# Two tiles on the path of each layer: residual through TensorE, statistics from PSUM, and a limit of two query projections in PSUM

## The chip, the cores and the metric

One core of one Trainium2 chip. The metric is the device time of one execution in microseconds (us), the median of several runs. A profile ("look") is one further execution, with its own span.

## The reference

Two layers, each an attention with feature maps (no square score matrix) and a gated feed-forward. S = 2048 rows are 16 tiles of 128; D = 576; 32 heads of 18; the feed-forward is 4608 wide.

```python
def A(x):                      # attention of one layer
    q, k, v = heads(layernorm(x) @ wqkv)
    pq, pk = q @ w_phi, k @ w_phi                       # per head, 18 x 18
    phi_q = concat(softmax(pq), softmax(-pq))
    phi_k = concat(softmax(pk), softmax(-pk))
    kv, z = phi_k^T v, sum(phi_k)                       # over ALL rows
    return (phi_q @ kv) / (phi_q @ z + 1e-6) @ wo
def B(x):                      # feed-forward
    n = layernorm(x); return ((n @ w_gate) * (n @ w_up)) @ w_down
for layer in range(2):         # the same weights in both
    x = x + A(x);  x = x + B(x)
```

The sum over all rows in `kv` is what makes a barrier: no row can finish its attention before the last row's key features are in. From there to the first feed-forward matmul only the first two tiles count, because a feed-forward block takes two tiles.

## The kernel before

The kernel is written as many small threads, each yielding operations for one engine. A list scheduler, run when the kernel is built, picks the next ready operation of each engine by priority. So a change of one thread can move the others. The parts that matter here:

```python
# a tile's query projection: a filler for TensorE; two PSUM banks each
def t_qproj(self, L, st_):
    ...
    if st_ >= s.pqn[L - 1]:                  # 16: never true
        yield ("when", lambda: s.sc.open)
    gots = yield ("acqn", ["pb"], 2, True)   # two PSUM banks
    banks = [g_[1] for g_ in gots]
    yield from s.proj(st_, s.Wq, "Wq", banks)
    ... two ScalarE copies, banks given back ...

# key-value sums of layer 2: three groups, one bank asked for at a time
def t_kv(self, b):
    ...
    for bi in range(3):
        (_, bank), = yield ("acqn", ["pb"], 1)
        ... matmuls vx, dd -> bank;  DVE: kvacc += bank;  give bank back

# end of attention of a tile
def t_aout(self, L, st_):
    ...  # numerators: eT x BD; all three thirds of BD are waited for
    reads=[("eT", et)] + [("BD", bi) for bi in range(3)]
    ...  # DVE: den + 1e-6, 1/den, o = num / den, and 64 columns doubled
    ops.append(Op(130, ... tensor_copy(o[:, 576:640], o[:, 512:576]) ...))
    ...  # first two tiles: 5 transposes on TensorE, ScalarE copies them to oT
    yield from s.proj(st_, s.Wo, "Wo", banks, s.oT[:, oTb, :, :], ...)
    for h in range(2):    # residual on DVE
        ... tensor_tensor(xs, s.ps[:, bank, 0:288], xs, ALU.add) ...
    yield ("sig", ("x1", L, st_))
# then t_ln: bn_stats of x_sb (DVE), Ln and Exp for rstd (ScalarE), normalise
# (DVE, again 64 columns doubled), 5 transposes (TensorE), ScalarE copy to xT
```

The doubled columns exist because 576 is 4.5 times 128: a transpose of the last half block puts its 64 rows into both halves of the partitions, where the half-height matmuls of this kernel read them. "Half-height" is a matmul with 64 partitions on the contracting side; projections inside feed-forward blocks run in that form, 18 half-height matmuls in place of 10 full ones.

The names: DVE is VectorE; a "bank" is one of the eight PSUM buffers of the kernel's pool "pb", into which TensorE writes. Wq, Wk, Wv and Wo are weights, and "a Wq projection" is the multiplication of one tile by Wq. xT and oT are transposed tiles. kvacc gathers the key-value sums, BD is the matrix made of them, and the numerators are the matmuls with BD.

## Time and profile before

| | before |
|---|---|
| median of 3 runs | 1123.65 us (1119.85 to 1124.21) |
| span of the profiled run | 1118.2 us |
| TensorE busy | 1070.8 us, 96% |
| layer 1: numerators to first feed-forward matmul | 106.87 to 121.26 |
| layer 2: first Wq after the last down projection, first numerator, first feed-forward matmul | 620.16, 646.86, 659.52 |

In profile lines a row of the timeline is: start, duration, engine, line of the kernel, operation, output<-inputs, shapes, count; in square brackets the idle time of that engine just before, and what ended it. PEld is the weight load of TensorE. Rows of the busy table by stretches are: stretch, its length, busy us and instruction count of PE, PEld, DVE, ACT, POOL, then granted clock, DMA share, GB/s.

### The profile page before, as it was taken

Reading aid. Unit: us, or ns where it says so; the run is one execution under the profiler, and the core shown is the slowest. Engines: PE = TensorE matmul, PEld = TensorE weight load, DVE = VectorE, ACT = ScalarE, POOL = GpSimd, SP = SyncE. Lnnn points to the kernel's source line nnn. Section 1 sums busy time; section 2 is a strip of 40 time slices with the busy share of each in tenths; the row PEclk is TensorE's granted clock in tenths of the full one; section 3 lists DMA queues with packets and bytes.
Section 4 is the critical chain, followed back from the end, with each engine's and each line's share of the span. In section 5 each row is a group of like instructions: output and inputs, shape, how many; then the busy total and the mean of one; then the engine's idle time right before and its main releaser. Section 6 shows DMA issues by size and latency. Waiting matters only on the chain.

```text
span 1118.2 us, 33702 instructions
## 1 busy us (share of the span) xinstructions
PE 1070.8 (96%) x15258; PEld 832.8 (74%) x15320; DVE 596.7 (53%) x1206; ACT 375.1 (34%) x859; POOL 313.5 (28%) x333
## 2 busy tenths in 40 slices
PE   5787999999999999999999889999999999999998
PEld 3565786868687786869687668696969696969685
DVE  7898754647466564646453576453535353524231
ACT  6776631414233242414232443131313130402120
POOL 5595522414242432413220234121212030300000
PEclk9799999999999999999999999999999999999999
DMA  7952127273452626371523202727172726352504
GB/s 188 250 225 64 29 41 204 47 203 47 142 102 76 161 37 190 45 203 26 162 65 105 88 13 54 217 36 214 35 201 48 202 47 188 61 178 50 177 28 139
DMA packets 181034, 128.23 MB, mean 115 GB/s; under 512 B 99354, under 2 KB 179738, under 8 KB 179738
## 3 DMA queue, kind: packets, MB, share of 16 engines
q1 hardware_dynamic: 180890, 126.07, 43.6%
q8 instruction: 120, 1.97, 0.7%
q14 instruction: 24, 0.20, 0.1%
HBM read 100.73 MB, written 2.36 MB: 92 GB/s over the span
## 4 chain that ended last, share of the span: by engine, by line
PE 82%; DVE 11%; ACT 4%; DMA 1%; issue 1%; POOL 0%; SPq 0%; DVEq 0%; ACTq 0%
PE ps L1342 47%; PE ps L1412 21%; PE ps L943 6%; PE ps L1415 4%; PE ps L931 2%; DVE ss L1058 2%; PE ps L1230 1%; DVE dd L990 1%; PE ps L1111 1%; DVE hT L1390 1%; ACT hT L1388 1%; DVE mxmn L976 1%; DVE st L877 1%; DVE mxmn L971 1%; DVE x_sb L1278 1%
## 5 line engine op out<-in xcount | busy, mean ns | idle before, releaser
L1342 PE MATMUL ps<-xT,Wu 64*128 64x256 bf16 x4608 | 581.6, 269 | 0.2 <-DVE hT L1390 0.2
L1342 PE MATMUL ps<-xT,Wg 64*128 64x256 bf16 x4608 | 580.5, 269 | 0.8 <-ACT xT L913 0.8
L1342 PEld LDWEIGHTS ps<-xT,Wu 64*128 64x128 bf16 x4608 | 431.1, 94 | 23.7 <-DVE hT L1390 2.2
L1342 PEld LDWEIGHTS ps<-xT,Wg 64*128 64x128 bf16 x4608 | 426.8, 94 | 27.6 <-issue 3.3
L1388 ACT CAST hT<-ps 128x512 bf16<-128x512 f32 x288 | 168.3, 585 | 566.5 <-PE ps L1342 537.2
L1390 DVE TENSOR_TENSOR hT<-ps,hT 128x512 bf16<-128x512 f32 x288 | 196.9, 690 | 214.9 <-ACT hT L1388 214.2
L1412 PE MATMUL ps<-wdr,hT 128*128 128x512 bf16 x913 | 237.5, 380 | 0.2
L1342 PE MATMUL ps<-xT,Wr 64*128 64x256 bf16 x1152 | 188.4, 269 | 0.0
L1415 PE MATMUL ps<-wdr,hT 128*128 128x64 bf16 x960 | 185.0, 193 | 2.8 <-issue 0.3
L1069 POOL TENSOR_TENSOR dd<-dd,ss 128x576 bf16<-128x576 bf16 x118 | 137.1, 1185 | 142.8 <-ACT ss L1065 131.5
L1412 PEld LDWEIGHTS ps<-wdr,hT 128*128 128x128 bf16 x960 | 93.9, 98 | 109.8 <-DMA wdr<-in_B_w_down_dram 1.4
L1040 POOL TENSOR_TENSOR dd<-xT,mxq 128x576 bf16<-128x576 bf16 x56 | 63.9, 1164 | 312.3 <-DVE mxq L1036 312.3
L1437 DVE TENSOR_TENSOR x_sb<-ps,x_sb 128x512 bf16<-128x512 f32 x32 | 22.0, 687 | 225.7 <-PE ps L1415 225.7
L903 POOL TENSOR_SCALAR xln<-x_sb,nmean,rstd 128x576 bf16<-128x576 bf16 x104 | 62.9, 610 | 171.6 <-ACT rstd L892 112.3
L1058 DVE TENSOR_REDUCE ss<-dd 128x64 f32<-128x1152 bf16 x61 | 82.1, 1348 | 23.7 <-ACT dd L1052 23.6
L1415 PEld LDWEIGHTS ps<-wdr,hT 128*128 128x128 bf16 x960 | 94.1, 98 | 0.0
L1342 PEld LDWEIGHTS ps<-xT,Wr 64*128 64x128 bf16 x1152 | 81.6, 94 | 5.4
L1050 ACT ACTIVATE dd<-dd 128x576 bf16<-128x576 bf16 x61 | 41.8, 685 | 51.4 <-DVE dd L990 31.7
L877 DVE BATCH_NORM_STATS2 st<-x_sb 128x6 f32<-128x288 bf16 x128 | 49.3, 447 | 4.1 <-DMA x_sb<-in_A_x_dram 3.8
L1412 PE MATMUL ps<-wdx,hT 128*128 128x512 bf16 x177 | 50.8, 380 | 0.0
L981 POOL TENSOR_TENSOR dd<-psb,mxmn 128x576 bf16<-128x576 bf16 x24 | 28.0, 1166 | 75.7 <-DVE mxmn L971 75.7
L943 PE MATMUL ps<-Wo,oT 64*128 64x288 bf16 x504 | 43.5, 283 | 0.9 <-DVE dd L1246 0.2
(113 smaller groups left out, 971.1 us busy)
## 6 DMA issues: line engine op xcount, KB each, us to landing
wdr<-in_B_w_down_dram SPq DMA_DIRECT2D x240, 288.0 KB, 3.6
wdx<-in_B_w_down_dram SPq DMA_DIRECT2D x48, 288.0 KB, 3.5
Wg<-in_B_w_gate_dram SPq DMA_DIRECT2D x4, 1152.0 KB, 15.9
Wu<-in_B_w_up_dram SPq DMA_DIRECT2D x4, 1152.0 KB, 18.1
x_sb<-in_A_x_dram SPq DMA_DIRECT2D x8, 288.0 KB, 3.4
out_dram<-x_sb SPq DMA_DIRECT2D x16, 144.0 KB, 2.6
Wraw<-in_A_wqkv_dram SPq DMA_DIRECT2D x8, 144.0 KB, 3.1
xT<-xln SPq DMA_TRANSPOSE x58, 2.7
```

What stands on the lines that cost most here:

```text
L877: ops.append(Op(d_dve(288), (lambda e, j=j, h=h: e.bn_stats(st[:, sl[j], 6 * h:6 * h + 6], x_sb[:, ss[j], 288 * h:288 * h + 288])), reads= ...
L903: em = [(lambda e, j=j, a=a, b=b, c=c: e.tensor_scalar(xln[:, sl[j], a:b], x_sb[:, ss[j], c:c + b - a], s.nmean[:, sl[j]:sl[j] + 1], rstd[ ...
L943: out.append(Op(61, (lambda e, h=h, k=k, st=(i == 0 and k == 0), sp=(i == 1 and k == 3): e.matmul(s.ps[:, banks[h], 0:N], L[r, k, :], Wm[r ...
L1040: yield ("ops", "pool", [Op(1150, (lambda e, d=d, mb=mb: e.tensor_tensor(d, p3, mb, ALU.subtract)), reads=[("xT", st_), ("mq", mq, br)], w ...
L1050: yield ("ops", "act", [Op(590, (lambda e: e.activation(de2, de2, ACTF.Exp, scale=-1.0)), reads=s.ddk(sm, 1), writes=s.ddk(sm, 1))])
L1058: Op(1320, (lambda e: e.tensor_reduce(ss[:, sm, :].rearrange("p (b g) -> p b g", b=2), e4, AX.X, ALU.add)), reads=s.ddk(sm, 0) + s.ddk(sm, ...
L1069: yield ("alt", [(eng, [Op(dur, (lambda e, ev=ev, rb=rb: e.tensor_tensor(ev, ev, rb, ALU.mult)), reads=s.ddk(sm, br) + [("ss", sm)], write ...
L1342: out.append(Op(54.3, (lambda e, bank=bank, cs=cs, lhsT=lhsT, rhs=rhs, st=st, sp=sp: e.matmul(ps[:, bank, cs].rearrange("p (a n) -> p a n" ...
L1388: yield ("ops", "act", [Op(540, (lambda e, gb=gb, p=p: e.copy(hT[:, p, :], ps[:, gb, :])), reads=[("gu", gb)], writes=[("hT", p)] + (s.raw ...
L1390: yield ("ops", "dve", [Op(625, (lambda e, ub=ub, p=p: e.tensor_tensor(hT[:, p, :], ps[:, ub, :], hT[:, p, :], ALU.mult)), reads=[("gu", u ...
L1412: ops.append(Op(d_pe(512), (lambda e, lhsT=lhsT, bank=bank, slot=slot, fi=fi, f=f: e.matmul(ps[:, bank, 0:512], lhsT, s.wslot(slot)[:, fi, ...
L1415: ops.append(Op(d_pe(64) + 3, (lambda e, lhsT=lhsT, sl=sl, slot=slot, fi=fi, f=f: e.matmul(ps[:, Z, 64 * sl:64 * sl + 64], lhsT, s.wslot(s ...
```

## The change

Its intent: shorten the chain of the first two tiles between the barrier and the feed-forward. (a) The residual is added by TensorE: two identity matmuls put x into the PSUM banks and Wo accumulates on top. (b) The statistics are read from PSUM, while ScalarE copies the sum to x. (c) The 64 columns are no longer doubled; instead the last transpose is done twice, into each half of the partitions. (d) 1/den may be formed on ScalarE as Exp(-Ln(den)), if the scheduler finds that sooner. (e) A numerator waits only for its third of BD. (f) At most two query projections may hold PSUM banks.

```diff
+        self.NPQ = 2
+        sc.pool("pq", self.NPQ)
 def t_qproj
-        if st_ >= s.pqn[L - 1]:
-            yield ("when", lambda: s.sc.open)
+        tok = yield ("acq", "pq")
         gots = yield ("acqn", ["pb"], 2, True)
 [...]
+        yield ("rel", "pq", tok)
 def t_ln
+                if banks is None: src = x_sb half
+                else:             src = s.ps[:, banks[h], 0:288]   # [condensed]
+                ... bn_stats(st[...], src)
 [...]
+    blocks5 = [(k, 0, 128, 128 * k + 128) for k in range(4)] + [(4, 0, 64, 576), (4, 64, 128, 576)]
 def t_aout
-                reads=[("eT", et)] + [("BD", bi) for bi in range(3)], ...
+                reads=[("eT", et), ("BD", k // 3)], ...
+        alts = [("dve", den)]
+        if st_ < 2:
+            lnd = [... Ln of den + 1e-6 ...]; lnd.append(... Exp, scale=-1.0 ...)
+            alts.append(("act", lnd))
+        yield ("alt", alts)
-        ops.append(Op(130, (lambda e: e.tensor_copy(o[:, 576:640], ...
+        if st_ >= 2:
+            ops.append(Op(130, (lambda e: e.tensor_copy(o[:, 576:640], ...
 [...]
+        if st_ < 2:
+            for h in range(2):
+                ... e.matmul(s.ps[:, bank, 0:288], s.ident[:], s.x_sb[half h], start=True, stop=False)
+            for h in range(2):
+                yield from s.proj(st_, s.Wo, "Wo", banks, ..., h, False)   # accumulate on it
+            yield ("sig", ("xp", L, st_))
+            for h in (1, 0):
+                ... e.copy(xs, s.ps[:, bank, 0:288]) on ScalarE ...
+            yield ("wait", ("bn", ...));  give the banks back
```

## The prediction

> **What bounds the kernel now.** I read the page first (busy shares, chain that ended last), then the busy table by stretches, then the timeline of the two stretches in which TensorE is not full, and last the waits of TensorE.

> From the page:

> ```profile
> span 1118.2 us, 33702 instructions
> ...
> PE 1070.8 (96%) x15258; PEld 832.8 (74%) x15320; DVE 596.7 (53%) x1206; ACT 375.1 (34%) x859; POOL 313.5 (28%) x333
> ...
> PE 82%; DVE 11%; ACT 4%; DMA 1%; issue 1%; POOL 0%; SPq 0%; DVEq 0%; ACTq 0%
> ```

> TensorE is busy for 96% of the span and carries 82% of the chain: the gated feed-forward blocks (L1342, L1412, L1415) run wall to wall. The 11% of DVE lies before about 121 us and around 620 to 660 us: the two places where an attention stage ends and the first block must wait for its two tiles. The busy table by stretches (columns: stretch, its length, then busy us of PE, PEld, DVE, ACT, POOL, granted clock, DMA share, GB/s) gives their size:

> ```profile
> 105.08:121.26 16.18, 13.52 (x132) 10.03 (x130) 13.38 (x35) 7.98 (x20) 2.16 (x2) 1.00 0.26 82
> 620.09:659.52 39.43, 31.30 (x276) 23.05 (x275) 29.25 (x68) 21.45 (x56) 9.95 (x8) 1.00 0.07 22
> ```

> TensorE idles 16.18 - 13.52 = 2.7 us in the first and 39.43 - 31.30 = 8.1 us in the second. The change touches only these, so **10.8 us (1.0%) is the ceiling** of what it can remove; what TensorE does there besides the chain (query projections, "Wq") is work that must be done anyway. The timeline of the first stretch (start, us, engine, line, instruction, idle before) shows the chain:

> ```profile
> 109.28 0.18 DVE L1248 COPY dd<-dd 128x64 bf16<-128x64 bf16 x1
> ...
> 110.26 0.69 ACT L1260 COPY oT<-ps 128x640 bf16<-128x640 bf16 x1 [0.93 <-PE ps L1257]
> ...
> 111.14 1.39 PE L931 MATMUL ps<-Wo,oT 128*128 128x288 bf16 x10 [0.92 <-ACT oT L1260]
> ...
> 112.56 0.46 DVE L1278 TENSOR_TENSOR x_sb<-ps,x_sb 128x288 bf16<-128x288 f32 x1 [0.15 <-PE ps L931]
> ...
> 113.05 0.82 DVE L877 BATCH_NORM_STATS2 st<-x_sb 128x6 f32<-128x288 bf16 x2
> ...
> 114.78 0.76 DVE L903 TENSOR_SCALAR xln<-x_sb,nmean,rstd 128x576 bf16<-128x576 bf16 x2
> ...
> 118.42 0.45 PE L911 MATMUL ps<-ident,xln 128*128 128x128 bf16 x5
> 118.71 2.61 PE L931 MATMUL ps<-Wq,xT 128*128 128x288 bf16 x20
> ```

> Each tile goes divide, transpose, copy (oT), Wo, residual on DVE, statistics, normalise, transpose. The last line matters: two Wq projections stand between the last transpose and the first feed-forward matmul at 121.26. In the second stretch there is one more thing, seen in the waits of TensorE (waits, in us: total, times, longest):

> ```profile
> PE ps L931 <- ACT oT L1260: 3.3, 4, 0.9
> PE ps L911 <- DVE xln L903: 3.0, 4, 1.1
> ...
> PE ps L1111 <- DVE kvacc L1154: 1.5, 2, 0.7
> ```

> The three key-value sums of layer 2 share one PSUM bank, and each waits 0.73 us for DVE to empty it.

> [...] here PE says 96% and PEld 74%, so I count idle stretches. [...] the normalisation costs 0.43 us for 576 columns and still 0.31 for the 64 doubled ones.

> **The change part by part.** I compared the built order of instructions of both kernels with their semaphores. Up to the end of layer 1's key-value sums (105.1 us) TensorE's order is the same.

> Removed per tile: the doubled columns after the division (0.18) and in the normalisation (0.31 to 0.33); two residual adds on DVE (2 x 0.46). Added per tile: two identity matmuls of 288 columns (2 x 0.123 us, from 20 such matmuls in 2.45 us) and one more transpose (0.06); two ScalarE copies of a 288-column half (0.41 each, from L1024). In all 8 identity matmuls (1.0 us) and 10 transposes (0.6, with the two tiles at the start of layer 2): 1.6 us of TensorE, partly in idle time. Statistics from PSUM should cost what they cost from SBUF (0.45). **1/den on ScalarE never happens**: the built order has no such instruction on ScalarE in any of the four tiles, so this part is worth nothing.

> Layer 1, walked with the durations above. The first numerator no longer waits for all of BD (L1175), it starts at 106.7 instead of 106.87 and ends 107.37 (before 107.55). Division ends 109.08, no copy follows (before 109.46). The second numerator has its own banks now and ends 109.27 (before 109.94). Transpose to 109.6, oT to 110.33, Wo 110.37 to 111.7 (before 112.52). Second oT to 112.87, its Wo 113.04 to 114.4 (before 114.98). First tile: ScalarE copy of half 1 to 112.18, its statistics to 112.62, mean to 112.86; rstd waits behind the other copy on ScalarE, 113.8; normalised at 114.25 (before 115.54). Transposed, two projections (2.46 us) follow to 117.15. Second tile normalised at 116.95 (before 118.37), transposed to 117.5, then one projection instead of two: feed-forward at **118.75 instead of 121.26: 2.5 us**. One projection has moved into the feed-forward block, where 18 half-height matmuls of it take 0.61 + 0.49 = 1.10 us (from 10 and 8 such matmuls of L943 at 159.89 and 161.59). Net **1.4 us**.

> Layer 2. Because only two projections may hold banks, the order after the first transpose (623.4) is Wk, not 20 Wq matmuls: Wk waits for the xT copy and starts at 624.3 instead of 626.17; the second tile's Wk at 628.1 instead of 632.4. DVE becomes the limit: tile 0's softmax subtraction ends 628.7 (before 630.23), tile 1's 634.1 (before 636.47), and the last POOL multiply ends 639.15 instead of 641.55: 2.4 us. The three sums now go to three banks, so both 0.73 us waits fall: BD ready at 642.85 instead of 645.9. First numerator ends 643.5 (before 647.53, where a projection pair lay before it), division 645.2 (before 649.24). From Wo (646.5) the walk is that of layer 1, without the last projection: feed-forward at **about 654.6 instead of 659.52: 4.9 us**. Two projections have moved into the feed-forward: -2.2. Net **2.7 us**.

> Sum: 1.4 + 2.7 = **4.1 us**, 38% of the ceiling. 1123.65 - 4.1 = 1119.5 us.

> **The rivals.** (1) *The new ScalarE copies become the wait.* In the built order the copy of tile 0's second half stands before the logarithm that makes rstd: 0.4 us of delay that I counted; if statistics from PSUM are slower too (0.6 instead of 0.45), each tile loses another 0.3, and the gain falls to about 3 us (1120.7). Against it: ScalarE is busy for only 7.98 of 16.18 us. (2) *The moved projections cost more inside the blocks than they gave.* They cost ScalarE copies beside the hT copies, three banks' rotation is tight there (2 x 3 banks for the pairs, 2 left). For it: already before, 108 / 18 = six Wq projections lay in blocks (L943). If they also stall TensorE, the gain is 1 to 2 us (1122). (3) *All idle time goes.* If the list scheduler's new order filled the gaps, 10.8 - 1.6 = 9.2 us: 1114.4. Against it: oT and xT copies (0.7 us each) remain on the path with nothing to fill them. (4) *Nothing is left of it*: a later DMA or block-to-block wait takes it back. The last 450 us are one PE chain, so a block that starts earlier ends earlier.

> **Range and chances.** The before runs lie at 1119.85, 1123.65, 1124.21, with 1119.98 for the profiled one: two levels 4 us apart, as large as the effect. So the range is the gain of 1 to 8 us widened by a level: 1114.5 to 1123. Over 2% (22 us) is twice the ceiling, and so is only left to a clock surprise; 22 us slower has no mechanism.

> **What would show it.** In the after profile: the first L1342 matmul near 118.8 and the second layer's first near 654.6; idle time of TensorE in the two stretches near 1.4 and 5 us; no L1154 waits; statistics from PSUM near 0.45 us; three Wq projections moved, that is 54 half-height matmuls more and 30 full ones fewer; no Ln/Exp of den on ScalarE. The prediction is wrong if the stretch starting at the first feed-forward block grows by more than the 1.1 us of each moved projection, if statistics or copies from PSUM take over 0.6 us, or if the feed-forward blocks themselves (11.8 us for 216 matmuls) slow down.

## The result, and the profile after

The kernel after takes **1116.14 us** (median of 4 runs, 1114.43 to 1116.64); the kernel before in the same rounds 1123.38 (1119.85 to 1124.21). The ratio is 0.9939, with a 95% interval from 0.9915 to 0.9962: surely a little faster. A ratio here is the mean time of one kernel's fast runs over that of the other's of the same rounds, so not quite the ratio of the medians quoted.

The page of the kernel after:

```profile
span 1114.3 us, 33775 instructions
...
PE 1072.3 (96%) x15300; PEld 837.1 (75%) x15362; DVE 592.0 (53%) x1190; ACT 376.5 (34%) x867; POOL 311.5 (28%) x332
...
PE 82%; DVE 9%; ACT 4%; DMA 2%; issue 1%; POOL 1%; SPq 0%; DVEq 0%; ACTq 0%
```

The span is 3.9 us shorter, TensorE's busy time 1.5 us longer, and DVE's share of the chain two points lower. The busy table by stretches of the kernel after: the first stretch of before, layer 1's first feed-forward block, layer 2's stretch and its first block.

```profile
105.10:121.26 16.16, 15.11 (x169) 11.75 (x167) 11.54 (x28) 10.31 (x27) 4.57 (x4) 1.00 0.25 82
119.11:165.46 46.35, 46.13 (x811) 41.24 (x812) 26.97 (x49) 21.62 (x49) 17.85 (x18) 1.00 0.27 42
620.41:654.74 34.33, 28.90 (x266) 22.24 (x265) 26.54 (x59) 20.05 (x52) 9.57 (x8) 1.00 0.09 28
654.74:697.43 42.69, 42.53 (x757) 37.16 (x759) 26.41 (x49) 19.16 (x43) 17.20 (x18) 1.00 0.29 46
```

The same two blocks in the kernel before:

```profile
121.26:165.95 44.69, 44.64 (x793) 39.67 (x794) 26.19 (x49) 21.12 (x46) 18.43 (x19) 1.00 0.28 43
659.52:700.87 41.35, 40.77 (x720) 35.50 (x722) 26.68 (x50) 16.52 (x35) 18.25 (x18) 1.00 0.25 47
```

In layer 1 TensorE now idles 16.16 - 15.11 = 1.05 us where it idled 2.7. In layer 2 the stretch is 34.33 us instead of 39.36, with 5.4 us idle instead of 8.1. Both first blocks are longer, by 1.66 and 1.34 us: 18 and 36 more half-height Wq matmuls, one and two moved projections, are in them (90 against 72, 36 against 0). In the second block TensorE idled 41.35 - 40.77 = 0.58 us before, and 0.16 us after.

The first tile's chain in layer 1, timeline of the kernel after:

```profile
109.47 0.42 PE L1299 MATMUL ps<-x_sb,ident 128*128 128x288 bf16 x2
...
110.35 1.40 PE L945 MATMUL ps<-Wo,oT 128*128 128x288 bf16 x10 [0.46 <-ACT oT L1281]
...
111.30 0.46 DVE L889 BATCH_NORM_STATS2 st<-ps 128x6 f32<-128x288 f32 x1
...
111.79 0.40 ACT L1308 CAST x_sb<-ps 128x288 bf16<-128x288 f32 x1 [1.19 <-PE ps L945]
...
112.22 0.47 DVE L889 BATCH_NORM_STATS2 st<-ps 128x6 f32<-128x288 f32 x1 [0.47 <-ACT x_sb L1308]
...
113.67 0.43 DVE L917 TENSOR_SCALAR xln<-x_sb,nmean,rstd 128x576 bf16<-128x576 bf16 x1 [0.56 <-ACT rstd L906]
...
114.82 2.62 PE L945 MATMUL ps<-Wq,xT 128*128 128x288 bf16 x20
```

The identity matmuls (0.42 us from 109.47) are over at 109.89, ScalarE's copy of oT, for which Wo waits, at 110.30 (0.69 us from 109.61), so they cost the chain nothing. Statistics from PSUM take 0.46 and 0.47 us, the second half after a wait of 0.47 us for ScalarE's copy of that half. The last line is the new wait: two Wq projections stand ahead of the second tile's transposes, which begin at 117.28.

For comparing kernels I use three lengths from each trace. "Layer 1" runs from the first BD write to the first down projection; "layer 2" from the first Wq after the last down projection of layer 1 to the first down projection of layer 2. Each thus contains the stretch and the block into which projections may move. "Numerator" is the start of layer 2's first numerator matmul after the start of the stretch.

| | before | after |
|---|---|---|
| layer 1 | 60.85 | 60.38 |
| layer 2 | 80.71 | 77.02 |
| numerator | +26.70 | +22.18 |

The sum falls by 0.47 + 3.69 = 4.16 us. A second look of each kernel gave 60.84 and 80.71 before, 60.39 and 76.86 after, so these lengths repeat to about 0.15 us.

### The profile page after: what moved, and what is told of

The parts are those of the page before. It is cut to its first block, busy times and chain, and to the rows that moved or that the text cites. A ratio compares the mean times of both kernels' runs of the same rounds, so it can differ in the third digit from the quotient of the medians.

```text
span 1114.3 us, 33775 instructions
## 1 busy us (share of the span) xinstructions
PE 1072.3 (96%) x15300; PEld 837.1 (75%) x15362; DVE 592.0 (53%) x1190; ACT 376.5 (34%) x867; POOL 311.5 (28%) x332
## 4 chain that ended last, share of the span: by engine, by line
PE 82%; DVE 9%; ACT 4%; DMA 2%; issue 1%; POOL 1%; SPq 0%; DVEq 0%; ACTq 0%
PE ps L1383 46%; PE ps L1453 20%; PE ps L957 6%; PE ps L1456 4%; PE ps L945 3%; DVE ss L1072 2%; PE ps L1244 1%; DVE dd L1004 1%; PE ps L1125 1%; ACT hT L1429 1%; DMA oT<-dd 1%; DVE hT L1431 1%; DMA wdr<-in_B_w_down_dram 1%; DVE mxmn L990 1%; DVE mxmn L985 1%
## 5 line engine op out<-in xcount | busy, mean ns | idle before, releaser
L1383 PEld LDWEIGHTS ps<-xT,Wu 64*128 64x128 bf16 x4608 | 431.7, 94 | 22.6 <-DVE hT L1431 1.6
L1453 PEld LDWEIGHTS ps<-wdr,hT 128*128 128x128 bf16 x960 | 93.8, 98 | 109.6 <-DMA wdr<-in_B_w_down_dram 1.0
L889 DVE BATCH_NORM_STATS2 st<-x_sb 128x6 f32<-128x288 bf16 x120 | 46.0, 445 | 3.7 <-DMA x_sb<-in_A_x_dram 3.6
```

The lines of the kernel that those rows point to most:

```text
L889: ops.append(Op(d_dve(288), (lambda e, j=j, h=h, src=src: e.bn_stats(st[:, sl[j], 6 * h:6 * h + 6], src)), reads=rd, writes=[("st", sl[j], ...
L1383: out.append(Op(54.3, (lambda e, bank=bank, cs=cs, lhsT=lhsT, rhs=rhs, st=st, sp=sp: e.matmul(ps[:, bank, cs].rearrange("p (a n) -> p a n" ...
L1453: ops.append(Op(d_pe(512), (lambda e, lhsT=lhsT, bank=bank, slot=slot, fi=fi, f=f: e.matmul(ps[:, bank, 0:512], lhsT, s.wslot(slot)[:, fi, ...
```

## The experiments

Twelve kernels in three batches (a, b, c), each batch on one chip, with 5 rounds. All outputs are right. Every row shows the median of the timed runs, the ratio to before in the same rounds with its interval, and the three lengths. In the looks of the last batch (c), the first four matmuls of each down projection are on record and in the earlier ones they are not (160 of them against 156 in 18.30 us), so that blocks end 0.22 us sooner there; 0.22 us is added to their lengths. "Half clock" is the clock time lost in those stretches (length times one less the granted clock).

| run | what | us | ratio | layer 1 | layer 2 | numerator | half clock |
|---|---|---|---|---|---|---|---|
| b1 | before, again | 1120.42 | 0.9985 (0.9969-1.0001) | 60.84 | 80.71 | +26.69 | 0 |
| a1 | after, again | 1116.15 | 0.9950 (0.9933-0.9966) | 60.39 | 76.86 | +22.18 | 0 |
| a2 | before + limit of two alone | 1115.93 | 0.9950 (0.9933-0.9968) | 60.75 | 76.89 | +22.36 | 0 |
| a3 | after without the limit | 1122.49 | 1.0010 (0.9992-1.0028) | 61.41 | 79.21 | +26.58 | 0 |
| a4 | after, residual on DVE | 1118.28 | 0.9966 (0.9948-0.9985) | 61.68 | 77.46 | +22.18 | 0 |
| b2 | after, all of BD waited for | 1116.82 | 0.9949 (0.9931-0.9967) | 60.74 | 76.86 | +22.19 | 0 |
| b3 | after, columns doubled | 1116.91 | 0.9952 (0.9936-0.9968) | 59.87 | 77.04 | +22.37 | 0 |
| b4 | after, 1/den on ScalarE | 1125.92 | 1.0032 (1.0012-1.0052) | 65.43 | 80.86 | +22.19 | 3.4 and 1.7 |
| c1 | a2, kv sums in one bank | 1120.78 | 0.9989 (0.9975-1.0002) | 60.75 | 81.18 | +24.70 | 0 and 3.4 |
| c2 | before, kv sums in three banks | 1120.00 | 0.9979 (0.9967-0.9991) | 60.85 | 79.06 | +24.88 | 0 |
| c3 | b3, last softmax multiply split | 1115.72 | 0.9942 (0.9930-0.9954) | 59.87 | 76.87 | +22.19 | 0 |
| c4 | after, limit of one | 1124.85 | 1.0027 (1.0011-1.0044) | 62.45 | 80.90 | +22.14 | 1.7 and 1.7 |

**The theory** after the result: the limit (f) carries the gain, nearly all of it in layer 2, by giving TensorE's order and PSUM's banks back to the path; the rest of the change is within 1 us. **The rival**: the shorter chain (a to c) carries it, and the limit only adds.

### b1, the kernel before again, and a1, the kernel after again

No edit. They measure how far looks and timed runs of one kernel differ.

> The kernel before itself, for a second trace of it. The timed runs give the limit alone and the whole change 5.6 us, the traces only 3.9 to 4.4, and the one trace of before is among its fastest runs (1120.0 of 1119.3 to 1124.6). If the spread is waits for data (transfers) that fall differently in each run, this trace has a span above 1119 us and one or more feed-forward stages 0.3 to 1 us longer than in the first trace, the two transition stretches unchanged (16.2 and 39.4 us). If the spread is of another kind (the granted clock), all stages are longer in proportion.

> The changed kernel itself, paired with the kernel before on one chip. Theory (the gain is what the two transition stretches lose, 2.15 + 5.06 us in the traces, less what the moved projections add to the feed-forward blocks, 3.3): about 4 us, ratio 0.9965, with the first feed-forward matmul at 119.1 us and the layer-2 stretch 34.4 us again. Rival (something outside these stretches also changed, as the timed runs of 1116.1 against 1123.4 suggest): ratio 0.9935 again, 7 us.

Measured: the three lengths of both repeat. The timed ratio of b1 to the same kernel is 0.9985, with 1 just inside its interval: so up to 0.15% (1.7 us) is noise, and the looks' spans are no better (1118.2 and 1117.1). My expectation for b1's span and its repeated transfer waits was not met: single stalls of 0.1 to 1.1 us in later feed-forward blocks come and go between looks of one kernel. They are chance and no part of the argument.

### a2, the limit of two alone

```diff
 (on the kernel before)
+        sc.pool("pq", 2)
-        if st_ >= s.pqn[L - 1]:
-            yield ("when", lambda: s.sc.open)
+        tok = yield ("acq", "pq")
+        yield ("rel", "pq", tok)
```

> The kernel before with the limit of two query projections alone. Theory (the limit moves Wk forward and gives the three key-value sums three banks, 3.9 of the 5.06 us of layer 2): layer-2 stretch 35.5 to 36.5 us instead of 39.4, first feed-forward matmul near 120.0 us, total 1.5 to 3 us better than before. Rival (the residual on TensorE and the statistics from PSUM bring the gain): layer-2 stretch above 38.5 us and the total within 0.7 us of before.

Measured: 1115.93 us, within noise of the whole change; layer 2 is 76.89 against 77.02, layer 1 60.75 against 60.38. I had expected too little of it. The residual on DVE, the statistics from SBUF, the doubled columns are all still there, and nothing is missing. The rival falls. Wk of tile 1 and the rest of the last key-value sums in a2, whose stretch began at 620.28:

```profile
628.49 1.40 PE L933 MATMUL ps<-Wk,xT 128*128 128x288 bf16 x10 [0.81 <-ACT xT L915]
...
639.18 1.17 PE L1113 MATMUL ps<-vx,dd 128*128 128x152 bf16 x17 [1.75 <-POOL dd L1071]
```

Both are as in the kernel after, shown under a3 with the kernel before.

### a3, everything but the limit

```diff
 (on the kernel after)
-        self.NPQ = 2
+        self.NPQ = 8
```

> The changed kernel without the limit (eight). Theory: the layer-2 stretch goes back to 37.5 to 39 us, and in layer 1, where the second numerator is now ordered behind the first tile's Wo, the first feed-forward matmul comes no earlier than 119.5; total within 1.5 us of before. Rival: layer-2 stretch below 36.5 us and at least 3 us better than before.

Measured: 1122.49, ratio 1.001: nothing is left (its two layers are 0.9 us shorter than before's in the trace, which the timed runs don't show). Layer 2's first numerator is back at +26.58. The timeline shows why. Wk of tile 1 and the second kv group, first in the kernel before:

```profile
632.39 1.39 PE L931 MATMUL ps<-Wk,xT 128*128 128x288 bf16 x10
...
642.69 0.58 PE L1111 MATMUL ps<-vx,dd 128*128 128x152 bf16 x8 [0.73 <-DVE kvacc L1154]
```

In a3, whose stretch began 2.4 us later:

```profile
634.66 1.39 PE L945 MATMUL ps<-Wk,xT 128*128 128x288 bf16 x10
...
644.96 0.58 PE L1125 MATMUL ps<-vx,dd 128*128 128x152 bf16 x8 [0.73 <-DVE kvacc L1168]
```

And in the kernel after:

```profile
624.73 1.40 PE L945 MATMUL ps<-Wk,xT 128*128 128x288 bf16 x10 [0.81 <-ACT xT L927]
...
628.57 1.40 PE L945 MATMUL ps<-Wk,xT 128*128 128x288 bf16 x10 [0.81 <-ACT xT L927]
...
639.13 1.18 PE L1125 MATMUL ps<-vx,dd 128*128 128x152 bf16 x17 [1.61 <-POOL dd L1083]
```

Without the limit, projections fill TensorE and the banks first, and Wk stands behind them. With it TensorE waits 0.81 us for the copy of xT and then does Wk at once: an idle wait in place of useful work, and the path is 4 us sooner. The sums also no longer wait for one bank: 17 matmuls run in one go.

### a4, the residual left on DVE

```diff
 (on the kernel after)
-        if st_ < 2:            # seed and accumulate
+        if st_ < 0:
-                yield ("wait", ("xp", L, 0)) ... t_ln(..., s.xbank[(L, 0)])
+                yield ("wait", ("x1", L, 0)) ... t_ln(...)
```

> The changed kernel with the residual added on DVE and the statistics read from SBUF again, all else kept. Theory: each stretch loses 0.5 to 0.6 us against the changed kernel (tile 2 normalised at 117.3 instead of 116.85), so the whole is about 1 us slower than the changed kernel, still 3 us better than before. Rival (this part is the main one): layer-2 stretch above 36.5 us, 2.5 us or more slower than the changed kernel.

Measured: 1118.28; 1.30 us longer in layer 1 and 0.44 in layer 2 than after, by one look of each. So with the rest of the change in place, the residual through TensorE gains 1.7 us. Yet a2 has its residual on DVE too and loses nothing. The first block of a4 holds 108 half-height Wq matmuls in its trace, after's and a2's 90, and it is 47.79 us long against 46.35 and 46.18. The loss in layer 1 came with one more projection moved into the block; the gain of this part alone isn't a property of it but of the schedule around it.

### b2, b3, the dependency on BD and the doubled columns

```diff
 (b2, on the kernel after)
-                reads=[("eT", et), ("BD", k // 3)], ...
+                reads=[("eT", et)] + [("BD", bi) for bi in range(3)], ...
 (b3, on the kernel after)
-    blocks5 = [... 4 full blocks ...] + [(4, 0, 64, 576), (4, 64, 128, 576)]
+    blocks5 = [(k, 0, 128, 128 * k + 128) for k in range(5)]
+    (and the two copies of 64 columns again)
```

> The changed kernel with every numerator matmul waiting for all three parts of BD, as before; its order of instructions is the same. Theory: the first numerator of layer 1 starts at 106.87 instead of 106.51 on the same scale (0.36 us), layer 2's by 0.3 us; the whole is 0.4 to 0.8 us slower than the changed kernel in the trace, inside the noise of the timed runs. Rival (this part is what the rest of the change is worth, so that the whole falls to the limit alone or below): 1.5 us or more.

> The changed kernel with the doubled columns back (5 transposes, the second normalising instruction of 0.31 us and the copy of 0.18). Theory: each tile's chain is longer by 0.5 us, the two stretches together by 1.0 to 1.6 us (layer 1 from 12.6 us after the first numerator to 13.2, layer 2 from 34.3 to 35.1), the whole 1 us slower than the changed kernel. Rival (hidden behind the projections, worth nothing): both stretches within 0.2 us of the changed kernel.

Measured: waiting for all of BD costs 0.36 us in layer 1 and nothing in layer 2 (76.86). Doubling the columns again costs nothing either; layer 1 is even 0.51 us shorter (59.87). The theory for b3, a loss of about 1 us, failed. Six transposes take 0.56 us where five took 0.45, and there are four such groups in a layer: 0.44 us of TensorE, which is now the limit in layer 1. That fits the 0.51; it was not tried apart. Neither can be told from noise in the timed runs.

### b4, 1/den on ScalarE

After never takes this alternative: in its trace all of den is formed on DVE (64 additions, 32 reciprocals). To measure it, it is forced.

```diff
 (on the kernel after)
-            alts.append(("act", lnd))
+            alts = [("act", lnd)]
```

> The changed kernel with 1/den of the first two tiles forced onto ScalarE (Ln twice and Exp, some 0.27 us each, instead of 0.17, 0.17 and 0.35 on DVE). Theory: the chain of each tile is 0.2 to 0.3 us longer, and the scheduler now puts fewer projections in front of the feed-forward; the first feed-forward matmul comes earlier (near 117 us) but the block grows by the moved projections, and start plus block (to the first down-projection, 165.5 us) ends within 0.7 us of the changed kernel. Rival (ScalarE frees DVE and the chain gets shorter): start plus block at 164.8 us or less and the whole 1 us faster.

Measured: 1125.92, 9.8 us slower than after. Both theories were wrong by a wide margin. The first numerator is no later (+22.19), the stretches are as long as after's (34.50 against 34.33 in layer 2), but the blocks are longer, 51.35 and 46.36 us against 46.35 and 42.69. Part of that is moved projections (144 and 72 half-height Wq matmuls in them, against 90 and 36). The other part was in none of my theories: the busy table shows a granted clock of 0.95 in the first block. In slices of it TensorE ran at half clock from about 118.5 to 125.4 us.

### c1 and c2, the two effects of the limit taken apart

```diff
 (c1, on a2: the last tile pair's three kv sums share one bank)
+            if one is None:
                 (_, bank), = yield ("acqn", ["pb"], 1)
+                one = bank if b == NB - 1 else None
 (c2, on the kernel before: the last pair asks for three banks together)
+        if b == NB - 1:
+            got = yield ("acqn", ["pb"], 3)
```

> Before plus the limit of two query projections, but the three key-value sums of the last tile of layer 2 are held to one PSUM bank, as they were before. Theory: of the 4.3 us by which the limit alone brought forward layer 2's first numerator (+26.70 to +22.36 us after the stretch's start), 2.7 to 2.9 come from Wk no longer standing behind 20 to 30 Wq matmuls, and about 1.5 from the sums going to three banks, so that two waits of 0.73 us fall. Then here the first numerator is at +23.6 to +24.0, and the trace shows two waits of TensorE for kvacc of some 0.7 us again; layer 1 as with the limit alone. Rival: the banks don't matter, DVE sets the time anyway: numerator at +22.3 to +22.6. Third: Wk's place is all, with no wait at all. Time 0.8 to 1.5 us over the limit alone (theory), equal to it (rival).

> Before, with the one change that the last tile's key-value sums take three PSUM banks together. Theory: the second half of the same split: Wk of layer 2 starts as before (626.2 less the look's offset), the two 0.73 us waits for kvacc fall, and layer 2's first numerator is at +25.0 to +25.4 instead of +26.70; the time falls by 1 to 1.5 us, or less where the scheduler fills the gap with a Wq pair. Rival: three banks only come free together later (Wq pairs hold them): the sums start later by as much, numerator at +26.5 to +27.

Measured: c2's numerator is at +24.88, 1.8 us sooner than before (theory 1.3 to 1.7), with Wk unmoved (+6.0 and +12.2 us in both), and layer 2 is 1.65 us shorter. So three banks alone give 40% of the 4.3 us by which a2 brings the numerator forward; the remaining 2.5 us, by subtraction, come with Wk ahead of Wq. That is near the theory's 2.7 to 2.9.

c1's numerator is at +24.70, later than both theory and rival, and layer 2 took 81.18 us, more than before. The two waits of 0.73 us are there as expected, but they don't make 2.3 us. Busy table of c1 around them, two us a row:

```profile
638.00:640.00 2.00, 0.37 (x3) 0.18 (x3) 0.57 (x1) 0.13 (x1) 0.96 (x1) 1.00 0.00 0
640.00:642.00 2.00, 1.15 (x11) 0.92 (x12) 0.70 (x2) 0.00 (x0) 1.25 (x2) 0.57 0.00 0
642.00:644.00 2.00, 2.00 (x12) 1.47 (x11) 1.27 (x2) 0.00 (x0) 0.65 (x1) 0.50 0.00 0
...
646.00:648.00 2.00, 2.00 (x22) 1.83 (x20) 1.75 (x8) 0.00 (x0) 0.00 (x0) 0.72 0.00 0
648.00:650.00 2.00, 1.22 (x14) 0.90 (x12) 1.57 (x6) 1.15 (x3) 0.00 (x0) 1.00 0.00 0
```

and its timeline:

```profile
642.41 2.61 PE L933 MATMUL ps<-Wq,xT 128*128 128x288 bf16 x10
```

Ten Wq matmuls took 2.61 us where they take 1.40 elsewhere: the granted clock was 0.50 there. The clock time lost in these stretches is 1.7 or 3.4 us in every case, that is 3.4 or 6.8 us at half clock. No single long pause stands before it in c1: the longest idle time of TensorE ahead of it is 1.75 us. So I looked at how busy TensorE was over 3.4 us, the length of the shortest fall. The emptiest 3.4 us of TensorE in each layer's stretch and block:

| | layer 1 | layer 2 |
|---|---|---|
| before | 50% busy | 37% |
| c2 | 50% | 44% |
| a2 | 54% | 49% |
| after | 69% | 52% |
| c4 | 37%, clock fell | 31%, clock fell |
| c1 | 54% | 27%, clock fell |
| b4 | 22%, clock fell | 17%, clock fell |

Of these, all whose emptiest 3.4 us were 31% busy or less lost the clock, none above 37% did, and at 37% both happened. The clock records in the packed traces show more: in each of the 14 looks every fall of the clock lies on one grid of 3.413 us, every half-clock time but the one at the kernel's end is a whole number of such steps (3.41 to 13.65 us), and the grid begins elsewhere in each look (the first fall is at 13.72 us in before and at 13.97 in after). A step of that grid is called a window here; the emptiest 3.4 us need not be one. The window before the fall in c1, the one before the fall in layer 1 of c4, and the emptiest window in layer 2 of the kernel before:

```profile
636.88:640.29 3.41, 0.93 (x12) 0.52 (x11) 1.66 (x3) 1.19 (x4) 1.88 (x2) 1.00 0.00 0
...
116.81:120.22 3.41, 1.62 (x26) 1.28 (x28) 1.66 (x4) 2.79 (x7) 1.16 (x1) 1.00 0.00 0
...
641.76:645.17 3.41, 1.95 (x24) 1.45 (x23) 1.83 (x3) 0.00 (x0) 1.91 (x2) 1.00 0.00 0
```

TensorE was 27%, 48% and 57% busy: the clock fell after the first two and not after the third, where the grid cuts the stretch's emptiest 3.4 us (37%) in two. Counted over all 14 looks (windows at full clock, without the first and last 10 us), the clock fell after all 25 windows that were busy for less than 41.6%, after 10 of the 33 between that and 56%, and after none above. So in these traces the falls go with little busy windows; what decides between 41.6% and 56%, and what places the grid, is not shown. An estimate from the two traces, shifting the grid over layer 2: the kernel before has a window under 42% at 19% of the positions and one under half at 74%, the kernel after at none.

So c1 and b4 are theories of waits spoilt by a second effect, 3.4 us of lost clock time in layer 2 of c1 and in layer 1 of b4. Taking c1's ten Wq matmuls at 1.40 instead of 2.61, as an estimate, its numerator would be at about +23.5 or a little less (its sums ran partly at half clock too), near the expected 23.6 to 24.0; what the banks are worth on top of Wk's place (1.1 us, by that estimate) is therefore only roughly known.

### c4, a limit of one

```diff
 (on the kernel after)
-        self.NPQ = 2
+        self.NPQ = 1
```

> After with a limit of one query projection instead of two. Theory: what the limit does is keep Wq from standing ahead of the path, so one does it as well: layer 2 from its first Wq to its first feed-forward within 0.5 us of 34.3, first numerator within 0.3 of +22.2, layer 1's first feed-forward no later than 119.2; more projections land in the blocks (each 1.1 us longer), so the total from layer start to block end is within 1 us of after. Rival: with one only, TensorE has no filler for the copies' waits, and the sum of both layers' stretches and blocks is over 1.5 us longer than after's 137.3.

Measured: 1124.85, 8.7 us slower than after. The theory is right up to the numerator (+22.14) and for the first feed-forward matmul of layer 1 (119.17), and wrong on the total; the rival is right on the total but not on the place, as the stretches themselves are hardly longer (35.06 against 34.33 in layer 2). The loss against after is 2.1 us in layer 1, whose block lost 1.7 us of clock time and took in 10 full Wq matmuls; 2.5 us in the first down projection, which now holds 20 Wq matmuls; and 3.9 us in layer 2, of which 0.7 in the stretch, where 1.7 us of clock time were lost, and 3.1 in the block, which holds 90 half-height Wq matmuls instead of 36. A projection that doesn't fill an idle time must be done later at full price, and with only one let in ahead, the clock fell once in each layer here (1.7 us of clock time lost in each).

### c3, a version to beat both

In a2 and after, the last step ahead of the kv sums is a softmax multiplication of 1.73 us on GpSimd. c3 is b3 with that step split: GpSimd takes half of the heads of one branch, DVE the rest.

```diff
 (on b3, last two tiles only)
+            yield part("pool", 900, 1, 0, 16)
+            yield part("dve", 675, 0, 0, 32)
+            yield part("dve", 400, 1, 16, 32)
```

> After with doubled columns kept, and the last softmax multiplication of the tiles on the path, 1.73 us on GpSimd, split between GpSimd (16 heads of one branch) and DVE (the rest). Theory: after the limit, this multiply is the longest single step ahead of the key-value sums, so the split brings layer 2's first numerator from +22.37 to about +21.7, and layer 1's BD 0.5 us or more ahead (which looks alone blur by 1 us); the whole is 0.5 to 1.1 us faster than after's 1116.1 to 1116.9, that is 1115.5 to 1116. Rival: DVE, already the limit there, takes on what GpSimd gives up, numerator at +22.4 or later and time equal or longer.

Measured: 1115.72 us, the lowest median of all, though not to be told from after's 1116.14; the numerator at +22.19 instead of b3's +22.37, a fifth of a microsecond where 0.7 was expected. The timeline of b3 at that step:

```profile
636.65 0.76 DVE L1083 TENSOR_TENSOR dd<-dd,ss 128x576 bf16<-128x576 bf16 x1
...
636.69 1.73 POOL L1083 TENSOR_TENSOR dd<-dd,ss 128x576 bf16<-128x576 bf16 x1 [2.77 <-DVE ss L1076]
```

and of c3, with the same half-width instruction 4 us before it:

```profile
632.68 0.68 POOL L1085 TENSOR_TENSOR dd<-dd,ss 128x288 bf16<-128x288 bf16 x1
...
636.57 1.60 DVE L1085 TENSOR_TENSOR dd<-dd,ss 128x576 bf16<-128x576 bf16 x2
...
636.62 1.25 POOL L1085 TENSOR_TENSOR dd<-dd,ss 128x288 bf16<-128x288 bf16 x1 [3.26 <-DVE ss L1076]
```

GpSimd's half took 0.68 us beside DVE's subtraction from PSUM (dd<-ps,mxmn, at 632.52), and 1.25 where DVE's own two multiplications had begun 0.05 us before it. Those two took 1.60 us there, and 1.14 at 633.19, where GpSimd's half was nearly over. In b3 it is alike with whole tiles: GpSimd's multiplication took 1.73 us behind DVE's (above) and 1.17 at 632.75, where it began first; DVE's took 0.76 in the first case and 1.27 in the second. So in b3 each is longer where the other began first, though the profile lists no wait; the cause is not shown. In c3 the pair was over 1.60 us after its start, where 1.14 and 0.68 make 1.82, and in b3 after 1.77, where 0.76 and 1.17 make 1.93. So at once they took about nine tenths of their sum, and the split gained 0.17 us. The rival (DVE takes on what GpSimd gives up) was near the truth.

## Why the prediction was right, and where it was not

The time was 3.4 us under the predicted 1119.5 and inside the range; the timed gain was 7.2 us where 4.1 was predicted, the traces' 4.2. The steps:

- **The ceiling and the two stretches: right.** Outside them the feed-forward blocks of both kernels have the same lengths, but for the single chance stalls.
- **Start of the first feed-forward block, layer 1: 119.11, predicted 118.75.** The chain came out within 0.2 us at each step up to the first tile's normalisation, which ended at 114.10 (predicted 114.25). The 0.36 us are in the next step: the six transposes and two Wq projections were put at 0.45 and 2.46 us, so that they would be over at 117.15 (though the prediction's own line for two projections has 2.61); they took 0.56 and 2.62, and the second tile's transposes began at 117.28 though its data was ready at 116.84. TensorE, not DVE, is the limit of that stretch after the change.
- **Start in layer 2: 654.74, predicted 654.6.** Right in every step to 0.6 us: Wk at 624.73 and 628.57 (624.3, 628.1), POOL's last multiplication over at 639.07 (639.15), no wait for kvacc, BD ready at 642.34 (642.85). The count of moved projections was right too: 54 half-height Wq matmuls more (162 against 108) and 30 full ones fewer (230 against 260).
- **The net of each layer failed: 1.4 and 2.7 predicted, 0.47 and 3.69 measured; the sum, 4.1, was right by two opposite errors.** The mis-sized term is "one projection has moved: 1.10 us" and "two projections have moved: -2.2". Layer 1's block grew by 1.66 us: besides the projection, ten of its Wo matmuls begin 1.7 us earlier (at 141.13 instead of 142.81), wait 0.3 us for DVE, and take 1.19 us where they took 0.78. By the prediction's own sign of being wrong (a block that grows by more than 1.1 us for each moved projection) this step failed in layer 1. Layer 2's block grew by only 1.34: in the kernel before it held 0.58 us of idle time on TensorE, which the projections now fill (0.16 us left), and they added 1.76 us of busy time (42.53 - 40.77) instead of 2.2.
- **What 1/den on ScalarE is worth: right that it never happens.** That it would cost 9.8 us if it did was beyond the prediction.
- **Statistics from PSUM 0.46 to 0.47, copies 0.40 to 0.41: right.** From SBUF the statistics of a half take 0.45 (mean of 120 in after). Rival 1 (the copies become the wait) falls: the copy's 0.47 us of wait was in the walk already. Seeding the sum through an identity matmul works here: the outputs are correct, and the two matmuls took 0.42 us beside ScalarE's copy. Rival 2 (moved projections stall the blocks) has a part in layer 1 and none in layer 2. Rival 3 (all idle time goes) was nearer in the number, 1114.4, but falls: TensorE still idles 1.05 and 5.4 us in the stretches. Rival 4 falls too: the later blocks kept the gain.
- **What the prediction did not ask was which part carries the gain.** It described six parts at length. The experiments show that one line, the limit, carries all of it (a2), and that without it nothing remains (a3). The prediction had the mechanism, "because only two projections may hold banks, the order is Wk", under layer 2 only, and gave layer 1's gain to the shorter chain; all of layer 1's gain is 0.47 us, and a2's layer 1 is within 0.4 us of after's.

What stays open: the timed runs differ by 5.6 to 7.2 us, the trace's two layers by 4.2. Up to 1.7 us of that is the noise that b1 measured; the rest is not shown. Two things bear on it. Before the barrier, in the first 100 us, the clock time lost was between 3.4 and 11.9 us in these looks, again in steps of 1.7, and different in two looks of one kernel (8.5 and 5.1 for before, 10.2 and 8.5 for after); the first BD write of layer 1 lay between 103.3 and 106.6 us. That chance is nearly as large as the effect. And the granted clock of every timed run is on record. At 0.995 the spans of the kernel before are 1117.1 to 1118.8 us (6 runs) and those of after 1112.7 to 1115.5 (3 runs): their means are 3.8 us apart, near the trace's 4.2. The 7 runs of before at 0.989 or less took 1120.8 to 1124.1, and none of the ten of after lies below 0.990. So what the traces don't show goes with a lower clock in some runs of before. That it is lost in layer 2, where the estimate under c1 and c2 puts the kernel before at risk and after not, would fit, but is not shown: no timed run has a trace.
